# The first batch of a fused sketch attention and squared-ReLU FFN, prepared in another order

## The chip, the cores and the metric

The kernel runs on one core of one Trainium2 chip. The metric is the device time of one execution in microseconds. Three executions of the kernel before gave 197.81, 198.57 and 199.13 us; the median is 198.57.

## The reference

Attention with polynomial-sketch features, then a feed-forward layer on every token. B = 4 batches, 4 heads, 1088 tokens, head size 32, sketch size r = 8 (so 64 features), d_ff = 2048; all inputs are float32.

```python
def phi(x):
    a = np.einsum('rd,bhsd->bhsr', S1, x)
    b = np.einsum('rd,bhsd->bhsr', S2, x)
    return np.einsum('bhsi,bhsj->bhsij', a, b).reshape(*x.shape[:-1], r * r)
q_p, k_p = (phi(q), phi(k))
kv = np.einsum('bhsf,bhsd->bhfd', k_p, v)
z = np.sum(k_p, axis=2)
num = np.einsum('bhsf,bhfd->bhsd', q_p, kv)
den = np.einsum('bhsf,bhf->bhs', q_p, z)[..., None] + 1e-06
x = (num / den).transpose(0, 2, 1, 3).reshape(B * S, H * D)
h = np.maximum(x @ w_in, 0.0)
out = h * h @ w_out
```

## The kernel before

A batch of 1088 tokens is 34 tokens on each of 32 partition rows of a head; all four heads lie side by side on 128 partitions. Tokens are worked on in two groups of 512 (g = 0, 1) and a rest of 64. A group has four tiles t of 128 tokens.

**Attention of a group.** DVE turns k or q in 32x32 blocks (`turned`, L251; here with a strided output, so that a row of the result tile is token 4 s' + j). TensorE projects the turned tile with the sketches of all heads (`proj`, L265 into `ab_ps`): sixteen instructions for a group, since each float32 product is two passes and each tile two halves of 64 columns. ACT copies the factors to SBUF (`ab`, L275). `outer` (L347) multiplies the two factors into 64 features a head, on DVE or POOL (`ph_k`, `ph_q`). For k, features and v give the sums kv and z. For q, the features are turned on TensorE (`t_ps`, L1042) and evicted (`phTh`), and `numerators` (L265 into `nd`) multiplies them with the block-diagonal sums `kvbd`; its last column of each head is the denominator. `normalize` divides, scales each token by its largest value and gives x as float16 (`xs`); TensorE turns it (`x_ps`, L617) and ACT or DVE evicts it to `xT`.

**Sums.** There are two ways in the kernel. `Kv` (L389, first batch only) has the features stationary, 64 columns, and streams v with a column of ones beside it: kv and z come out in the place that `kvbd` needs, two ACT copies finish it. `KvRows` (L428, batches 1 to 3) has v stationary, 32 columns, and streams the features. Here z comes from 18 small products of the factors themselves (L447); kv and z then need further products (with the identity L478, with `pick` L485), ACT copies into `kvbd` (L492), and three DVE steps (`own_z` L497, L504).

**FFN.** The tokens of a group (a chunk) pass through 16 column blocks of w_in: `pg` (L906, float16, one pass), relu and square on DVE, ACT or POOL, then `po` (L994, float32, two passes) adds up over the 16 blocks. A finished `po` is turned back, scaled and stored (`store_gen`, L862; the store L886 is one SP transfer of 256 KB).

**Order.** The program of each engine is written out by hand. The first batch's first group is prepared line by line (L1003 to L1100); from there on `block` emits one `pg` and one `po` at a time, and `pump` lets the generators of the later work (`x_gen`, `batch_gen`, `second_gen`, `store_gen`) put their pieces between the blocks by estimated due times (`now` counts blocks). Each engine runs its own program in order. All loads and stores are on the SP queue, in order; for batches 1 to 3 q's factors pass through DRAM on it as well (`q_one`, `q_two`, `f`; L305 to L322), and POOL multiplies them to features (L332).

**PSUM.** Four tags of two banks each: `pg`, `po` and `ms` are two buffers, `nd` is one of double size. A tile of a tag waits until the readers of the tile that had the buffer are done.

**Zero products.** `idle_products(n)` (L237) issues n float16 products of zeros of 128x512 that nothing reads. In the preparation there are 17: six at the start, one behind the turn of the sketches (`s_ps`, L1005, from which DVE makes the projection weights `w_bd`, L1008), two ahead of the first group's sums, one between these and q's turn, two and five around the turn of the second group's q.

The preparation in its order on TensorE: zero products, `s_ps`, projections of k (two groups and the rest) and of q (group 0), sums of k group 0, turn of half of q's features, sums of group 1 and rest, turn of the other half, projection of q's group 1, numerators of group 0, turn of half of group 1's features, turns of `xs`, turn of the other half, first two `pg` (`first_two`, L931), numerators of group 1, two more `pg`, and the first `po`.

Of the kernel before, what the change touches and what calls it, by code (L numbers as in the profile page):

```python
# [21 lines left out]
def kernel(  # L22
# [32 lines left out]
    Identity = mybir.ActivationFunctionType.Identity  # L55
# [65 lines left out]
    def load_v(b, h, eng):  # L121
        eng.dma_start(
            v_sb[b][:, 256 * h : 256 * h + 256],
            bass.AP(
                v.tensor,
                v.offset + (b * H + h) * S * D,
                [[NM * D, 32], [8 * D, 4], [1, 256]],
            ),
        )

    def load_v_rest(b, i, eng):
        eng.dma_start(
            _v(v_rm[b // 2], 0, [[D, H], [1, D]], 64 * (b % 2) + 32 * i, 32),
            bass.AP(
                v.tensor,
                v.offset + (b * H * S + 32 + i) * D,
                [[NM * D, 32], [S * D, H], [1, D]],
            ),
        )
# [29 lines left out]
    for i in range(4):  # L169
        load_v(0, i, sp)  # L170
    load_q(0, 1)
    for i in range(2):
        load_v_rest(0, i, sp)
# [5 lines left out]
    for i in range(4):  # L179
        load_v(1, i, sp)  # L180
    for i in range(2):
        load_v_rest(1, i, sp)
# [9 lines left out]
    eps = cpool.tile([128, 1], F32)  # L192
    dve.memset(eps[:], 1e-6)
# [26 lines left out]
    def sum_constants():  # L220
        yield 1, 0
        dve.tensor_reduce(
            out=pick_s[:, :], in_=_v(iden, 0, [[1, 32], [32, 4]]), axis=AX, op=add
        )
        yield 1, 0
        pool.tensor_copy(
            out=_v(pick, 0, [[8, 32], [1, 8]]), in_=_v(pick_s, 0, [[1, 32], [0, 8]])
        )
        dve.tensor_reduce(
            out=_v(own_j, 0, [[8, 2], [1, 8]]),  # L230
            in_=_v(iden, 0, [[64, 2], [1, 8], [8, 8]]),
            axis=AX,
            op=add,
        )

# [10 lines left out]
    def turned(x, g, of_q=False):  # L246

        if g < 2:
# [3 lines left out]
                _v(xt, 0, [[128, 4], [1, 4], [4, 32]]), _v(x, c0, [[32, 4], [w, 4], [1, 32]])  # L252
# [16 lines left out]
    def proj(xt, ps_tag="ms"):  # L269
# [5 lines left out]
        act.copy(ab[:, :], ab_ps[:, :])  # L275
# [64 lines left out]
    def outer(ph, ab, t0, m, eng, a=None, g=None):  # L340


        if g is None:
            a, b, n, c0, c1 = ab if a is None else a, ab, 16, 64 * t0, 64 * t0 + 8
        else:
            a, b, n, c0, c1 = ab, ab, 8, 128 * g + 32 * t0, 256 + 128 * g + 32 * t0
        eng.tensor_tensor(  # L347
            out=_v(ph, 256 * t0, [[64, 4 * m], [8, 8], [1, 8]]),
            in0=_v(a, c0, [[n, 4 * m], [1, 8], [0, 8]]),
            in1=_v(b, c1, [[n, 4 * m], [0, 8], [1, 8]]),  # L350
            op=mult,
        )
# [11 lines left out]
    def proj_rests(xk, b, xqs, qf=None, ps_tag="ms"):  # L364
# [11 lines left out]
        for g, _ in xqs:  # L376
            act.copy(qf[64 * g : 64 * g + 64, 512:576], ab_ps[64 * g : 64 * g + 64, 64:128])

    def outer_rest(b, eng):
# [4 lines left out]
            in0=_v(ab, 0, [[8, 4], [1, 8], [0, 8]], p0, 64),  # L384
# [4 lines left out]
    class Kv:  # L389

        def __init__(self, b):
            self.b, self.n = b, 0
            self.ps = pspool.tile([128, 512], F32, name="kv_ps", tag="nd", bufs=1)

        def products(self, ph, c0, vt, v0, v1, one, p0=0, n=128):
            z = 64
            for h in range(H):
                off = v0 + v1 * h
                for f in range(0, 64, z):
                    x = 64 * (h % 2) + f  # L400
                    nc.tensor.matmul(  # L401
                        self.ps[x : x + z, 64 * (h // 2) : 64 * (h // 2) + 64],
                        ph[p0 : p0 + n, c0 + 64 * h + f : c0 + 64 * h + f + z],
                        _v(vt, off, [[one - off, 2], [1, D]], p0, n),
                        start=self.n == 0 and h < 2,
                        stop=False,
                        skip_group_check=True,
                    )
            self.n += 1

        def tiles(self, ph, g, ts):
            for t in ts:
                self.products(ph, 256 * t, v_sb[self.b], D * (4 * g + t), 256, VONE)

        def rest(self):
            r, p0 = self.b // 2, 64 * (self.b % 2)
            self.products(rest_ab[r][1], 0, v_rm[r], 0, D, H * D, p0, 64)

        def finish(self, engs):
            u = self.b  # L420
            for x in range(2):
                evict(
                    engs[x],
                    _v(kvbd[u], VW * x, [[2 * VW, 2], [1, VW]], 64 * x, 64),
                    _v(self.ps, 0, [[64, 2], [1, VW]], 64 * x, 64),
                )

    class KvRows:  # L428
# [3 lines left out]
        def __init__(self, b, abs_):  # L432
# [13 lines left out]
        def factors(self, ab, c0, c1, w, p0, n, first, last):  # L446
            nc.tensor.matmul(  # L447
                self.ps[32 * w : 32 * w + 32, 512:544],
                ab[p0 : p0 + n, c0 : c0 + 32],
                ab[p0 : p0 + n, c0 + c1 : c0 + c1 + 32],  # L450
                start=first,
                stop=last,
            )

        def products(self, phs):
            r, p0 = self.b // 2, 64 * (self.b % 2)
            for g in range(2):
                for t in range(4):
                    self.values(
                        phs[g], 256 * t, v_sb[self.b], D * (4 * g + t), 256,  # L460
                        0, 128, g + t == 0, False,
                    )
                for t in range(4):
                    self.factors(
                        self.abs, 128 * g + 32 * t, 256, t, 0, 128, g == 0, g == 1 and t > 0
                    )
            self.values(rest_ab[r][1], 0, v_rm[r], 0, D, p0, 64, False, True)
            self.factors(rest_ab[r][0], 0, 32, 0, p0, 64, False, True)
            rows = apool.tile([128, 64], F32, name="kvr", tag="kvr")
            sums = apool.tile([128, 32], F32, name="kvz", tag="kvz")  # L470
            act.copy(rows[:, :], self.ps[:, 0:64])
            act.copy(sums[:, :], self.ps[:, 512:544])
            self.rows, self.sums = rows, sums

        def spread(self):
            t_ps = pspool.tile([128, 512], F32, name="kvt_ps", tag="ms", bufs=2)
# [6 lines left out]
            for pr in range(2):  # L483
                for x in range(2):
                    nc.tensor.matmul(  # L485
                        t_ps[64 * x : 64 * x + 64, 64 + 16 * pr : 80 + 16 * pr],
                        pick[:, 128 * pr + 64 * x : 128 * pr + 64 * x + 64],
                        self.sums[:, 16 * pr : 16 * pr + 16],
                    )
            u = self.b  # L490
            for x in range(2):
                act.copy(  # L492
                    _v(kvbd[u], VW * x, [[2 * VW, 2], [1, D]], 64 * x, 64),
                    _v(t_ps, 0, [[D, 2], [1, D]], 64 * x, 64),
                )
            own_z = apool.tile([128, 32], F32, name="own_z", tag="own_z")
            dve.tensor_tensor(  # L497
                out=_v(own_z, 0, [[16, 2], [1, 16]]),
                in0=_v(t_ps, 64, [[16, 2], [1, 16]]),
                in1=_v(own_j, 0, [[0, 2], [1, 16]]),  # L500
                op=mult,
            )
            for x in range(2):
                dve.tensor_reduce(  # L504
                    out=_v(kvbd[u], VW * x + D, [[2 * VW, 2]], 64 * x, 64),
                    in_=_v(own_z, 0, [[16, 2], [1, 16]], 64 * x, 64),
                    axis=AX,
                    op=add,
                )

    def feature_t(ph, T, pr, eng):

        feat_until[0] = now[0] + 2
        t_ps = pspool.tile([128, 512], F32, name="t_ps", tag="ms", bufs=2)
        for t in range(T):
            nc.tensor.transpose(
                t_ps[:, 128 * t : 128 * t + 128],
                ph[:, 256 * t + 128 * pr : 256 * t + 128 * pr + 128],
                iden[:, :],
            )  # L520
        sb = apool.tile([128, 512], F32, name="phT", tag=f"phT{pr}", bufs=2)
        if eng is None:
            return sb, t_ps
        evict(eng, sb[:, 0 : 128 * T], t_ps[:, 0 : 128 * T])
        return sb

    def numerators(b, phT, by_pair=False):


        def cols(pr, t):  # L530
            if isinstance(phT[pr], tuple):
                return phT[pr][t // 2], 128 * (t % 2)
            return phT[pr], 128 * t

        nd = pspool.tile([128, 1024], F32, name="nd", tag="nd", bufs=1)
        steps = [(t, pr) for t in range(4) for pr in range(2)]
# [546 lines left out]
    for _ in range(2):  # L1083
        next(norm)
# [69 lines left out]
```

## Time and profile before

| | us |
|---|---|
| median of three executions | 198.57 |
| the profiled execution | 199.0 |
| its span | 197.2 |
| around the span | 1.8 |

| engine | busy us | share of the span | instructions |
|---|---|---|---|
| TensorE products (PE) | 191.5 | 97% | 1402 |
| TensorE weight loads (PEld, beside the products) | 102.7 | 52% | 1402 |
| DVE | 120.5 | 61% | 264 |
| ACT | 112.5 | 57% | 221 |
| POOL | 64.0 | 32% | 84 |

Busy time of PE is from the start of a product to its modelled end, and products overlap, so it says that the array is never long without work, not how fast it works. The speed is read from the distance of equal products. The costliest groups are the FFN's: 256 `po` instructions and 142 `pg`. In the chain that ended last, `po` has 56% of the span, `pg` 16%, `nd` 5%, `ab_ps` 3%. A timeline row is: start, duration, engine, line, operation, output and inputs, shapes, count; several instructions of a kind are one row. In brackets is the idle time of the engine ahead of it and what ended that.

### The profile page before, as it was taken

To read this page: it belongs to the slowest core of one execution; us is meant where nothing else is said; L and a number is where in the kernel's file an instruction comes from. 1 tells how busy PE (TensorE), PEld (TensorE's weight loads), DVE (VectorE), ACT (ScalarE), POOL (GpSimd) and SP (SyncE) were. 2 spreads that over 40 slices of the span, in tenths; PEclk is the share of its full clock that TensorE was granted. 3 is DMA by queue.
4 is the path that set the end of the run, shared out by engine and by line. 5 is a ranking of instruction groups with operands and counts; after the bars stand their busy time and mean duration, and the time that the engine had idled before them with its cause. 6 is when DMAs were issued, how large, how long until landed. Compare 5 with 4: busy or idle time off the path is not lost.

```text
span 197.2 us, 3669 instructions
## 1 busy us (share of the span) xinstructions
PE 191.5 (97%) x1402; PEld 102.7 (52%) x1402; DVE 120.5 (61%) x264; ACT 112.5 (57%) x221; POOL 64.0 (32%) x84
## 2 busy tenths in 40 slices
PE   7999999999999999999999999999999999999992
PEld 2784544555545454555554645455545444544791
DVE  4837897565587738547977264556387545545671
ACT  3235767663666666464757474557466656565570
POOL 3604224635245018241632271516313222222000
PEclk9999999999999999999999999999999999999999
DMA  5799840395990105982000159721000100100011
GB/s 159 217 341 326 279 128 2 83 269 165 267 327 34 56 3 130 294 240 99 2 5 0 55 118 303 193 98 53 2 0 3 53 0 0 53 0 2 0 57 27
DMA packets 13634, 21.91 MB, mean 111 GB/s; under 512 B 2672, under 2 KB 8048, under 8 KB 13616
## 3 DMA queue, kind: packets, MB, share of 16 engines
q1 hardware_dynamic: 13376, 21.60, 36.6%
q8 instruction: 11, 0.18, 0.4%
q10 hardware_dynamic: 240, 0.07, 0.2%
q14 instruction: 7, 0.06, 0.1%
HBM read 15.61 MB, written 6.06 MB: 110 GB/s over the span
## 4 chain that ended last, share of the span: by engine, by line
PE 94%; DMA 2%; DVE 1%; issue 1%; ACT 0%
PE po L994 56%; PE pg L906 16%; PE nd L265 5%; PE ab_ps L265 3%; PE kvr_ps L438 2%; PE po L953 2%; PE o_ps L871 2%; PE po_r L953 2%; DMA k_sb<-in_k_dram 2%; PE kv_ps L401 1%; PE x_ps L617 1%; PE ab_ps L282 1%; PE t_ps L1042 1%; PE idle_ps L240 1%; PE abr_ps L265 0%
## 5 line engine op out<-in xcount | busy, mean ns | idle before, releaser
L994 PE MATMUL po<-g,w_o 128*128 128x512 f32 x256 | 130.6, 592 | 0.0
L923 DVE TENSOR_SCALAR gt<-pg 128x512 f32<-128x512 f32 (+1 forms) x107 | 69.2, 651 | 52.5 <-PE pg L906 38.1
L926 ACT ACTIVATE g<-gt 128x512 f32<-128x512 f32 (+1 forms) x107 | 63.8, 598 | 58.8 <-DVE gt L923 56.4
L994 PEld LDWEIGHTS po<-g,w_o 128*128 128x128 f32 x256 | 48.5, 191 | 35.7 <-issue 19.2
L914 POOL TENSOR_TENSOR g<-gt 128x512 f32<-128x512 f32 x23 | 23.9, 1040 | 79.3 <-ACT gt L913 79.3
L906 PE MATMUL pg<-xT,w_in 128*128 128x512 f16 x126 | 47.8, 380 | 0.0
L906 PEld LDWEIGHTS <-w_in 128*128 128x128 f16 x142 | 13.8, 98 | 25.0 <-issue 24.1
L332 POOL TENSOR_TENSOR phF<-f,f 128x576 f32<-128x576 f32 (+1 forms) x12 | 16.1, 1364 | 12.8 <-DMA f<-q_two 12.8
L347 POOL TENSOR_TENSOR ph_k<-ab 128x512 f32<-128x512 f32 x14 | 14.5, 1070 | 10.1 <-ACT ab L288 8.8
L913 ACT ACTIVATE gt<-pg 128x512 f32<-128x512 f32 x23 | 13.4, 581 | 0.0
L879 DVE TENSOR_TENSOR o_sb<-o_ps,beta 128x512 f32<-128x512 f32 x8 | 5.5, 692 | 6.9 <-PE o_ps L871 6.9
L251 DVE STREAM_TRANSPOSE xt<-k_sb 128x512 f32<-128x512 f32 x8 | 8.6, 1117 | 1.7 <-DMA k_sb<-in_k_dram 1.7
L265 PEld LDWEIGHTS nd<-kvbd,phF 128*64 128x64 f32 x208 | 6.9, 137 | 4.5 <-issue 4.5
L251 DVE STREAM_TRANSPOSE xt<-q_sb 128x512 f32<-128x512 f32 x8 | 8.6, 1121 | 0.0
L265 PEld LDWEIGHTS ab_ps<-w_bd,xt 128*64 128x64 f32 x160 | 7.1, 163 | 2.5 <-issue 1.2
L265 PE MATMUL ab_ps<-w_bd,xt 128*64 128x64 f32 x160 | 7.5, 252 | 0.4 <-DVE w_bd L1008 0.4
L920 ACT ACTIVATE g<-gt 128x512 f32<-128x512 f32 x12 | 7.6, 630 | 0.4
L240 PE MATMUL idle_ps<-zero 128*128 128x512 f16 x17 | 6.6, 511 | 1.2 <-DVE own L198 1.2
L265 PE MATMUL nd<-kvbd,phF 128*64 128x66 f32 x208 | 7.7, 224 | 0.0
L919 ACT ACTIVATE gt<-pg 128x512 f32<-128x512 f32 x12 | 7.0, 587 | 0.0
L953 PE MATMUL po<-w_o,g 128*128 128x128 f32 x32 | 6.2, 278 | 0.0
L953 PE MATMUL po_r<-w_o,g 128*128 128x128 f32 x32 | 6.0, 275 | 0.0
(114 smaller groups left out, 143.4 us busy)
## 6 DMA issues: line engine op xcount, KB each, us to landing
q_two<-qf SPq DMA_DIRECT2D x8, 288.0 KB, 4.1
f<-q_one SPq DMA_DIRECT2D x4, 576.0 KB, 6.1
f<-q_two SPq DMA_DIRECT2D x4, 576.0 KB, 4.7
v_sb<-in_v_dram SPq DMA_DIRECT2D x16, 128.0 KB, 4.0
out_dram<-o_sb SPq DMA_DIRECT2D x8, 256.0 KB, 2.4
k_sb<-in_k_dram SPq DMA_DIRECT2D x3, 544.0 KB, 6.1
q_sb<-in_q_dram SPq DMA_DIRECT2D x3, 544.0 KB, 4.4
w_in<-in_moe_w_in_dram SPq DMA_DIRECT2D x2, 512.0 KB, 6.2
```

Source lines behind the costliest of these rows:

```text
L240: nc.tensor.matmul(idle_ps[:, :], zero[:, 0:128], zero[:, :])
L251: dve.transpose(_v(xt, 0, [[128, 4], [1, 4], [4, 32]]), _v(x, c0, [[32, 4], [w, 4], [1, 32]]))
L265: nc.tensor.matmul(out_ps[p0 + c : p0 + c + z, c0 : c0 + w], lhsT[:, l0 + c : l0 + c + z], rhs)
L332: pool.tensor_tensor(out=ph[:, c], in0=fs[g][0][:, c], in1=fs[g][1][:, c], op=mult)
L347: eng.tensor_tensor(out=_v(ph, 256 * t0, [[64, 4 * m], [8, 8], [1, 8]]), in0=_v(a, c0, [[n, 4 * m], [1, 8], [0, 8]]), in1=_v(b, c1, [[n, 4 ...
L906: nc.tensor.matmul(pg[:, 0:nt], w_in[:, 128 * c : 128 * c + 128], xT[:, 0:nt])
L913: act.activation(gt[:, 0:nt], pg[:, 0:nt], Relu)
L914: pool.tensor_tensor(out=g2[:, 0:nt], in0=gt[:, 0:nt], in1=gt[:, 0:nt], op=mult)
L923: dve.tensor_scalar(out=gt[:, 0:nt], in0=pg[:, 0:nt], scalar1=0.0, scalar2=None, op0=amax)
L926: act.activation(g2[:, 0:nt], gt[:, 0:nt], Square)
L953: nc.tensor.matmul(po[r][:, 0:128], g2[:, 128 * r : 128 * r + 128], w_o[:, 128 * c : 128 * c + 128], start=c == 0, stop=c == NC - 1,)
L994: nc.tensor.matmul(po[0][:, 0:nt], w_o[:, 128 * c : 128 * c + 128], g2[:, 0:nt], start=(c == 0), stop=(c == NC - 1),)
```

## The change

It rewrites the preparation of the first batch and, with it, the order of tokens inside a tile.

- Zero products: seven and two (for six and one) up to the first projection; the two and the one ahead of and between the sums are gone; four and two (for two and five) stand around the turn of the second group's first half.
- The first batch's sums are made by `KvRows`: z from the factors, picked out early (`pick_sums` into a tile of the tag `po`, `own_sums` on DVE), kv from 72 products with v stationary, then `turn` and `place`. The constants for it (`pick`, `own_j`) are made in the setup and no longer in a lane of the later work.
- ACT's copy of the factors puts the two factors apart (`ab`), as for the later batches. `outer` and `outer_rest` on DVE take one factor from PSUM.
- q is turned without stride: a row of the tile is token s' of 32, in four runs. So the store of a chunk becomes four transfers of 64 KB.
- The numerators of group 0 are two tiles, `nd` and `nd_b` (tag `pg`), and `normalize_first` works on both; the denominator's small sum is on DVE, where it was on ACT.
- Of group 1, only the first half of the features is turned ahead of the first FFN products; the second half is turned behind the first four, and its numerators are put into the stream of blocks by a lane that starts at block 2.
- Two of the four casts of w_in (for three) come ahead of the first FFN products.

```diff
@@ turned, proj
             dve.transpose(
-                _v(xt, 0, [[128, 4], [1, 4], [4, 32]]), _v(x, c0, [[32, 4], [w, 4], [1, 32]])
+                xt[:, :] if of_q else _v(xt, 0, [[128, 4], [1, 4], [4, 32]]),
+                _v(x, c0, [[32, 4], [w, 4], [1, 32]]),
             )
...
-        act.copy(ab[:, :], ab_ps[:, :])
+        act.copy(
+            _v(ab, 0, [[128, 2], [8, 16], [1, 8]]), _v(ab_ps, 0, [[8, 2], [16, 16], [1, 8]])
+        )
@@ sums
+    def factor_sums(ps, c0, ab, a0, a1, w, p0, n, first, last):
+        nc.tensor.matmul(
+            ps[32 * w : 32 * w + 32, c0 : c0 + 32],
+            ab[p0 : p0 + n, a0 : a0 + 32],
+            ab[p0 : p0 + n, a0 + a1 : a0 + a1 + 32],
+            start=first,
+            stop=last,
+        )
+    def pick_sums(t_ps, c0, sums):
+        for pr in range(2):
             for x in range(2):
+                nc.tensor.matmul(
+                    t_ps[64 * x : 64 * x + 64, c0 + 16 * pr : c0 + 16 + 16 * pr],
+                    pick[:, 128 * pr + 64 * x : 128 * pr + 64 * x + 64],
+                    sums[:, 16 * pr : 16 * pr + 16],
                 )
...
@@ normalize_first
+        for i, nd in enumerate(nds):
+            dve.tensor_reduce(
+                out=_v(top, 8 * i, [[4, 2], [1, 4]]),
+                in_=_v(nd, 0, [[256, 2], [VW, 4], [1, 32]]),
+                axis=AX, op=amax, apply_absolute_value=True,
+            )
+            dve.tensor_scalar(
+                out=den[:, 8 * i : 8 * i + 8], in0=_v(nd, D, [[256, 2], [VW, 4]]),
+                scalar1=1e-6, scalar2=None, op0=add,
+            )
+        dve.reciprocal(rden[:, :], den[:, :])
...
+        for i, nd in enumerate(nds):
             dve.tensor_tensor(
+                out=_v(xs, 256 * i, [[128, 2], [32, 4], [1, 32]]),
...
@@ store_gen
-        sp.dma_start(dst, o_sb[:, :])
+        for dst, p0, n, c0, w in dsts:
+            sp.dma_start(dst, _v(o_sb, c0, [[1, w]], p0, n))
@@ the preparation
-    idle_products(6)
+    idle_products(7)
     s_ps = pspool.tile([128, 16], F32, name="s_ps", tag="nd", bufs=1)
     nc.tensor.transpose(s_ps[:, :], s_nat[:, :], iden[0:16, 0:16])
-    idle_products(1)
+    idle_products(2)
...
-    xk.append(turned(k_sb[0], 2))
-    xq = turned(q_sb[0], 0, True)
     pk = [proj(xk[0], "pg"), proj(xk[1], "pg")]
-    proj_rests(xk[2], 0, [])
-    pq = proj(xq)
...
+    xkr = turned(k_sb[0], 2)
+    xq = turned(q_sb[0], 0, True)
     for g in range(2):
         outer(phk[g], pk[g][1], 0, 2, dve, pk[g][0])
         outer(phk[g], pk[g][1], 2, 2, pool)
-    idle_products(2)
-    kv0 = Kv(0)
-    kv0.tiles(phk[0], 0, range(4))
+    pq = proj(xq)
+    pkr = proj_rests(xkr, 0, [])
+    kv0 = KvRows(0)
+    for g in range(2):
+        for t in range(4):
+            factor_sums(kv0.ps, 512, pk[g][1], 32 * t, 128, t, 0, 128, g == 0, g == 1 and t > 0)
+    kv0.rest_sums()
+    kv0.keep_sums()
     outer(phq, pq[1], 0, 2, dve, pq[0])
+    outer_rest(0, dve, pkr)
     outer(phq, pq[1], 2, 1, dve, pq[0])
     outer(phq, pq[1], 3, 1, pool)
-    outer_rest(0, dve)
-    idle_products(1)
+    zt_ps = pspool.tile([128, 32], F32, name="zt_ps", tag="po", bufs=2)
+    pick_sums(zt_ps, 0, kv0.sums)
+    for g in range(2):
+        for t in range(4):
+            kv0.tile(phk[g], g, t)
+    own_sums(0, zt_ps, 0)
+    xq1 = turned(q_sb[0], 1, True)
...
-    turned_half(0, (act, act))
-    xq1 = turned(q_sb[0], 1, True)
-    kv0.tiles(phk[1], 1, range(4))
-    kv0.rest()
-    kv0.finish((act, act))
-    turned_half(2, (act, dve))
+    pqT = [turned_half(phq, 0, (act, act))]
+    kv0.rest(True)
+    kv0.keep_rows()
+    pqT.append(turned_half(phq, 2, (act, dve)))
+    kvt_ps = pspool.tile([128, 64], F32, name="kvt_ps", tag="pg", bufs=2)
+    kv0.turn(kvt_ps)
+    kv0.place(kvt_ps)
+    nd_b = pspool.tile([128, 512], F32, name="nd_b", tag="pg", bufs=2)
+    nd0 = [
+        numerators(0, pqT[0], None, range(2)),
+        numerators(0, pqT[1], nd_b, range(2, 4)),
+    ]
     pq1 = proj(xq1, "pg")
     phq1 = ph_tile("ph_q", 2)
-    outer(phq1, pq1[1], 0, 2, pool)
-    nd0 = numerators(0, pqT)
-    idle_products(2)
...
+    for t0 in (0, 2):
+        outer(phq1, pq1[1], t0, 2, pool)
...
+    idle_products(4)
+    pqT = [turned_half(phq1, 0, (act, act))]
+    idle_products(2)
+    chunk_of(0, 0, xT0, next(norm))
     first_two()
-    nd1 = numerators(0, pqT1, True)
+    nd1 = numerators(0, pqT[0], None, range(2))
     nd_taken[0] = True
     for _ in range(2):
         first_product()
-    act.copy(w_in[:, 1536:2048], w_in32[:, 1536:2048])
+    pqT.append(turned_half(phq1, 2, (act, dve)))
+    for c in range(2, 4):
...
+    def second_half():
+        numerators(0, pqT[1], nd1[:, 512:1024], range(2, 4))
+        yield 1, 0
+        yield from x_gen(0, 1, None, (), nd1)
+
+    lanes.append([second_half(), 2, 1])
...
-    lanes.append([x_gen(0, 1, None, (), nd1), 3, 1])
-    lanes.append([sum_constants(), 8, 0])
```

In `KvRows`, `tile` and `rest` are the 64 and 8 instructions of the 72, `rest_sums` the last factor sums, `keep_rows` and `keep_sums` ACT's copies of kv and z out of PSUM, `turn` the products with the identity and `place` ACT's two copies into `kvbd`.

## The prediction

> **What bounds it now.** I read the windows by stage first, then the chain of waits of the first 23 us, then the timeline of the same stretch by engine. The windows (stretch, its length, busy time and instructions of PE, PEld and so on) split the run in two:
>
> ```profile
> 0.00:19.00 19.00, 17.05 (x208) 10.85 (x208) 11.30 (x34) 6.88 (x18) 6.87 (x23) 1.00 0.83 257
> 21.10:60.00 38.90, 38.90 (x280) 19.55 (x280) 27.30 (x56) 24.40 (x48) 15.77 (x18) 1.00 0.63 186
> 130.00:170.00 40.00, 40.00 (x161) 19.43 (x160) 23.39 (x53) 24.24 (x43) 11.48 (x13) 1.00 0.04 14
> ```
>
> From the first `po` product (21.09) on TensorE has no hole; every other engine rests 30% of it or more. So that part is as long as its TensorE work, and the change can gain only where the first batch is prepared. The chain (start, us, what) shows that preparation:
>
> ```profile
> 5.09 2.10 PE ab_ps L265 x32
> 7.40 1.00 PE ab_ps L265 x16
> 8.40 0.97 PE idle_ps L240 x2
> 9.36 1.29 PE kv_ps L401 x32
> 10.65 0.32 PE idle_ps L240
> 11.41 1.46 PE kv_ps L401 x40
> 14.07 0.96 PE nd L265 x32
> 15.06 0.28 ACT small L560
> 19.04 0.59 PE pg L936 x2
> 19.63 1.08 PE nd L265 x32
> 21.25 0.92 PE po L994 x2
> ```
>
> Up to 15 us it runs through TensorE, zero products (`idle_ps`) included; then through DVE's normalization to the first FFN product at 19.04. TensorE's own timeline (start, us, engine, line) says at what speed:
>
> ```profile
> 1.19 2.74 PE L240 MATMUL idle_ps<-zero 128*128 128x512 f16 x6 [1.19 <-DVE own L198]
> ...
> 7.27 1.12 PE L265 MATMUL ab_ps<-w_bd,xt 128*64 128x64 f32 x16
> ...
> 13.39 0.69 PE L265 MATMUL ab_ps<-w_bd,xt 128*64 128x64 f32 x16
> ...
> 16.18 1.24 PE L240 MATMUL idle_ps<-zero 128*128 128x512 f16 x5
> ...
> 43.30 0.65 PE L438 MATMUL kvr_ps<-ph_k,v_sb 128*32 128x64 f32 x32
> ```
>
> Six zero products take 2.74 us at the start, five take 1.24 later; sixteen projection products take 1.12, later 0.69. The page's clock row shows full speed throughout, but the spacing says half speed at first. The products of `kv_ps` in windows of 0.2 us place the change at about 9.8:
>
> ```profile
> 9.48:9.68 0.20, 0.20 (x8) 1.00 0.82 164
> 9.68:9.88 0.20, 0.20 (x10) 1.00 0.91 225
> 9.88:10.08 0.20, 0.20 (x14) 1.00 0.64 205
> ```
>
> **The change, part by part.** *Zero products at the start.* Seven instead of six end at 1.19 + 7 x 0.43 = 4.2. The S transpose moves from 3.86 to 4.3 and is hidden: `w_bd` waits anyway for DVE's first transpose (4.84). Two zero products behind it end at 5.35, so the first projection starts at about 5.5 instead of 5.09: +0.4. What it may buy is the clock. Now TensorE pauses for about 1 us in all between 3.7 and 6.1; with the change for about 0.5. I take full speed at 6.4 (bounds: 5, and 9.8 as now).
>
> *To the features.* First projection 5.5 to 6.35 at half speed, plus 0.3 until its last result: ACT's copy 6.66 to 7.03 (now 6.26 to 6.63). POOL, which follows at once,
>
> ```profile
> 6.72 2.09 POOL L347 TENSOR_TENSOR ph_k<-ab 128x512 f32<-128x512 f32 x2 [1.25 <-ACT ab L275]
> 8.89 0.62 POOL L347 TENSOR_TENSOR ph_q<-ab 128x256 f32<-128x256 f32 x1
> ```
>
> then ends its two `ph_k` halves at 9.2 and its `ph_q` quarter at 9.9; 0.4 later than now. DVE is not later: it turns k and q until 7.07 now, and begins its first `ph_k` half there. The q turn without stride: the contiguous 128x64 k rest takes 232 ns, the strided q rest 232, the strided 128x512 turn 1121; nearest contiguous row of 512 columns is `gt`, 691. So 0.69 to 1.12; I take 0.7 as that row has the shape. Neither end enters the sum, because the first `ph_k` half waits for the copy at 7.03 in both, and the seven other q turns lie on an engine with a third of its time free. [...]
>
> Second projection at full speed 6.4 to 7.05, third 6.95 to 7.55 (0.69 each, row 13.39), copy at 7.95. DVE: `ph_k` 7.07 to 8.33 (1.26 as now), `ph_q` (0.63, then 0.37) and the rest (0.37) to 9.75, where now they end at 10.2. With the clock late: 10.3.
>
> *Sums.* Removed: 72 `kv_ps` products, 1.29 + 1.46 = 2.75 us, and three zero products (8.40 and 10.65, 1.29 us) in front of them. Added: 72 products with v stationary (two times 0.65, which overlap their neighbours: the whole group in batch 1 runs from 43.30 to 44.74, its 18 factor sums included: 1.44), 8 picking and 4 turning products (0.36 and 0.34 by batch 3's rows, tails included). The factor sums wait for ACT's copies (8.2), the picking for `keep_sums` (8.7); the 64 big ones run 9.0 to 9.9, behind the last `ph_k` half at 9.2. Then `ph_q`'s turn: its PSUM buffer is now the one of the q projection, so all of the DVE products at 9.75 must be over; start 10.1. From there 4 turns (0.44), 8 rest products, ACT's two evictions and `keep_rows` (0.65 + 0.21) to 11.4, `kv0.turn` to 11.85, two `place` copies (0.42) to 12.3. This last piece is new (before: two copies out of `kv_ps`). `own_sums` (0.19 + 2 x 0.18) and xq1's turn lie on DVE between 9.75 and 11.4, under ACT's chain; without that cover they cost up to 1.3. So the numerators start at 12.35 instead of 13.90; late clock 12.6.
>
> *Normalization.* `nd` in two tiles: the second half ends at 13.5 (half of 0.96 each); DVE starts its first reduction at 13.05. Left behind the last product: 0.42 reduction, 0.2, reciprocal and five small steps at 0.2 to 0.28 (now 16.04 to 17.15 for five of them), two `xs` halves at 0.4: 2.8, where now 15.03 to 18.28 = 3.25. `xs` is complete at 16.35. On TensorE xq1's projection now follows the numerators: copied at 14.4, so POOL's two products (1.06 and 1.07) are at 15.5 and 16.6. The turn of the first half and two zero products stand before the `xs` turns, so these start at 16.55, 0.2 behind `xs`. Evictions as now (0.37, 0.29), first FFN product at 17.35: -1.7.
>
> *Behind it.* Now 2.05 us pass from there to the first `po`, filled by 32 numerators; then 16 numerators, two products that wait for their buffers (relu at 1.3 us behind the first product) and the second half's turns (0.44), 2.3 us: first `po` at 19.65, -1.45. The 16 numerators left are moved into block 2, where TensorE is the bound: half of 1.08, plus about 0.1 (a group of 32 adds 1.19 between blocks at 50.85 to 52.26): +0.65. Sum: -1.45 + 0.65 = **-0.8**; late clock -0.55.
>
> *Stores, loads and constants.* Eight stores of 0.59 us issue time become 32; a piece costs 0.35 to 0.59 (shortest and ordinary SP rows), so a store takes 0.8 to 1.8 us longer on SP. Behind the one at 44.12 stand the second group's factor transfers: `f` lands at 51.3 + 4.7 = 56.0 and POOL uses it at 57.92; 1.9 us of cover, then 1.2 more until the numerators at 61.96. Costed at nothing; with the cover gone up to 1. The last store is `o_row`, unchanged. Picking constants lie in DVE's wait for k (1.71 us before 3.90, they take 0.74).
>
> **Rivals** (times from the profiled 199.0). *The clock falls back* (slower). Between 7.5 and 12.3 TensorE would have about 2.3 us of work, 48%, and no zero products; the emptiest stretch at full speed now, 15 to 19, has some 55%, five zero products among it. For it: lower than anything the trace shows held. Against: no pause is longer than about 1 us. It decides if the array is slow again at the numerators: these and turns +1.2, then blocks of 1.07 at double length. The start needed 8.6 us of mixed work to reach full speed; 2 to 4.3 us of loss: +2.4 to +4.7 net, 201.4 to 203.7. [...]
>
> *A wait at block 2.* The moved numerators need ACT's eviction of the second half, queued behind two squares: ready at about 21.5, TensorE there at 21.6. Half to one us late, with all later `po` queued behind: -0.3 to +0.2, 198.7 to 199.2.
>
> *Clock at 5:* the first projection too is full speed, POOL 0.35 earlier: -1.1 to -1.3, 197.7 to 197.9.
>
> **Numbers.** The profiled execution took 199.0 (span 197.2, 1.8 around it); the median shown is 198.57, so against the median every result lies 0.43 lower. Forecast 0.52: 198.57 - 0.7 (between -0.55 and -0.8) = 197.9, own range 197.4 to 198.4. Wait at block 2: 0.2. Early clock: 0.15. Clock falling back: 0.13 by the trace (almost all that is over 1% slower). Range 196.9 to 199.8: the early clock with the early end of its terms, and the wait with a store's lost cover. About 1% (2 us) is what can be told from no change. Faster by more needs nearly three times my sum: 0.08; slower 0.12.
>
> **What would show it.** Right: first projection near 5.5 with sixteen products in 0.7 us by the second; numerators near 12.4, first FFN product near 17.4, first `po` near 19.7, no holes after. Wrong: `po` pitch over 1.07 near 20 (clock), idle TensorE before the numerators in block 2, DVE still busy with `own_sums` or xq1 at 12.3, or POOL waiting for `f` near 58.

## The result and the profile after

The changed kernel takes 199.31 us (median of 20 executions, 199.01 to 199.71); the kernel before, measured beside it, 197.81 (20 executions, 197.52 to 199.28). The ratio is 1.0062, with a 95% interval of 1.0047 to 1.0077: 0.6% slower, where 0.35% faster was forecast. (It is the ratio of the means, 199.31 and 198.08. The medians lie further apart, because the kernel before has a group of six executions above 198.3 and fourteen at 197.98 or below.) The profiled execution of the changed kernel took 199.55, its span is 197.8. (Executions more than 1.5% above the fastest of their kernel are left out of all ratios here, but not out of medians.)

TensorE's timeline after (start, duration, engine, line, operation, output and inputs, shapes, count, and in brackets the idle time ahead with what ended it) has these rows for the steps that the prediction names:

```profile
5.47 2.26 PE L257 MATMUL ab_ps<-w_bd,xt 128*64 128x64 f32 x48
...
12.66 0.69 PE L257 MATMUL nd<-kvbd,phTh 128*64 128x66 f32 x16 [0.53 <-ACT kvbd L487]
...
15.52 0.39 PE L231 MATMUL idle_ps<-zero 128*128 128x512 f16 x1 [0.48 <-issue]
...
17.42 0.61 PE L575 MATMUL x_ps<-iden,xs 128*128 128x128 f16 x4 [0.43 <-DVE xs L564]
18.51 0.59 PE L942 MATMUL pg<-xT,w_in 128*128 128x512 f16 x2 [0.47 <-DVE xT L76]
...
20.53 1.02 PE L1000 MATMUL po<-g,w_o 128*128 128x512 f32 x2
...
22.56 1.02 PE L257 MATMUL nd<-kvbd,phTh 128*64 128x66 f32 x16
```

The preparation did become shorter than in the first profile: the first `po` starts at 20.53, where it was 21.09. But more than half of the 1.24 gained up to the numerators (12.66, before 13.90) is lost again between them and the first FFN product (18.51, before 19.04: 0.53 left), and the rest at the 16 numerators in block 2 (blocks are counted from 0, so this is the third). There are 128 blocks of the kind `po`, of two instructions each. Setting the first instruction of each against that of the same block in the first profile gives -0.55 for the first block, -0.62 for the second, +0.44 for the third and +0.48 for the last. So the 125 blocks behind the third, with all the stores in four pieces, lost 0.04 together.

The normalization is seen in DVE's timeline after:

```profile
14.89 0.17 DVE L549 TENSOR_REDUCE mm<-small 128x4 f32<-128x16 f32 x1
15.10 0.77 DVE L553 TENSOR_SCALAR mp<-mm 128x4 f32<-128x4 f32 x1
15.91 0.18 DVE L556 RECIPROCAL rm<-mp 128x4 f32<-128x4 f32 x1
16.12 0.79 DVE L557 TENSOR_TENSOR small<-small,rm 128x16 f32<-128x16 f32 x1
```

and POOL's timeline over the same stretch has this row for its two products:

```profile
14.78 2.09 POOL L344 TENSOR_TENSOR ph_q<-ab 128x512 f32<-128x512 f32 x2 [5.01 <-ACT ab L267]
```

Two steps of 128x4 and 128x16 elements take 0.77 and 0.79 us, while steps of the same size next to them take 0.17 or 0.18. The first ends (15.87) where POOL's first product ends (15.85), the second (16.91) where POOL's second does (16.87). The bracket of neither row names a wait: it lies inside the duration. In the profile before, the first of these steps (`mp`) lay between POOL's two products and took 0.17:

```profile
16.73 0.17 DVE L578 TENSOR_SCALAR mp<-mm 128x4 f32<-128x4 f32 x1
```

```profile
14.57 1.06 POOL L347 TENSOR_TENSOR ph_q<-ab 128x512 f32<-128x512 f32 x1 [5.05 <-ACT ab L275]
...
17.13 1.07 POOL L347 TENSOR_TENSOR ph_q<-ab 128x512 f32<-128x512 f32 x1
```

### The profile page after: what moved, and what is told of

The parts are those of the page before. It is cut to its first block, busy times and chain, and to the rows that moved or that the text cites. A ratio compares the mean times of both kernels' runs of the same rounds, so it can differ in the third digit from the quotient of the medians.

```text
span 197.8 us, 3764 instructions
## 1 busy us (share of the span) xinstructions
PE 190.1 (96%) x1430; PEld 101.3 (51%) x1430; DVE 119.7 (61%) x267; ACT 113.0 (57%) x224; POOL 63.9 (32%) x84
## 4 chain that ended last, share of the span: by engine, by line
PE 92%; DVE 3%; ACT 1%; issue 1%; POOL 1%
PE po L1000 55%; PE pg L912 15%; PE nd L257 4%; PE ab_ps L257 3%; PE kvr_ps L433 3%; PE idle_ps L231 2%; PE po L959 2%; PE o_ps L876 2%; PE po_r L959 2%; PE ab_ps L276 1%; PE x_ps L620 1%; PE t_ps L1058 1%; PE kvt_ps L479 1%; POOL g L950 1%; DVE small L538 0%
## 5 line engine op out<-in xcount | busy, mean ns | idle before, releaser
L231 PE MATMUL idle_ps<-zero 128*128 128x512 f16 x15 | 6.0, 530 | 1.7 <-DVE own L195 1.2
L257 PEld LDWEIGHTS ab_ps<-w_bd,xt 128*64 128x64 f32 x160 | 6.5, 152 | 2.0 <-issue 0.9
L257 PE MATMUL ab_ps<-w_bd,xt 128*64 128x64 f32 x160 | 6.5, 237 | 0.0
L876 PEld LDWEIGHTS o_ps<-iden,oT 128*128 128x128 f32 x32 | 3.9, 141 | 3.9 <-issue 2.9
```

Source lines behind the costliest of these rows:

```text
L231: nc.tensor.matmul(idle_ps[:, :], zero[:, 0:128], zero[:, :])
L257: nc.tensor.matmul(out_ps[p0 + c : p0 + c + z, c0 : c0 + w], lhsT[:, l0 + c : l0 + c + z], rhs)
```

## The experiments

In each profile the trace records from when on TensorE's clock is granted in full; "onset" is that time. With it go the starts of the first numerators, of the first FFN product and of the first `po`.

| kernel | onset | numerators | `xs` complete | first FFN product | first `po` | span |
|---|---|---|---|---|---|---|
| before, first profile | 9.78 | 13.90 | 18.28 | 19.04 | 21.09 | 197.2 |
| before, again | 4.96 | 13.11 | 17.48 | 18.24 | 20.29 | 196.4 |
| before, zero products 7 and 2 | 6.42 | 12.54 | 16.91 | 17.67 | 19.72 | 195.9 |
| after | 6.91 | 12.66 | 17.69 | 18.51 | 20.53 | 197.8 |
| after, again | 6.12 | 13.11 | 18.14 | 18.96 | 20.98 | 198.2 |
| after, second product on DVE | 6.00 | 12.56 | 16.98 | 17.80 | 19.94 | 197.0 |
| after, xq1 early | 6.76 | 12.60 | 16.78 | 18.22 | 20.24 | 197.5 |
| after, both | 4.30 | 12.37 | 16.18 | 17.14 | 19.28 | 196.4 |
| after, operands in PSUM | 6.85 | 12.63 | 16.45 | 17.76 | 19.78 | 197.0 |
| after, evictions exchanged | 6.02 | 12.86 | 17.89 | 18.71 | 20.73 | 197.6 |
| after, zero products 6 and 1 | 5.26 | 12.61 | 17.64 | 18.46 | 20.49 | 197.7 |
| all cures | 6.96 | 12.81 | 16.65 | 21.30 | 23.36 | 199.7 |
| all cures, loads later | 5.14 | 13.04 | 16.88 | 17.86 | 19.91 | 196.1 |
| the same, v rest first | 4.78 | 12.31 | 16.15 | 17.43 | 19.48 | 195.6 |

**The kernel before once more** (no edit).

> The kernel before, unchanged, for a second profile of it. Theory A (the profile that the prediction was made from shows a late run): in about two of three executions TensorE reaches full speed well ahead of 9.8 us, the numerators start near 12.9 and the span is near 196.0. Rival B: the executions differ elsewhere (transfers, end), and the start looks as in the first profile (full speed near 9.8, numerators 13.9) whatever the span.

It took 198.21. TensorE's timeline:

```profile
13.11 1.11 PE L265 MATMUL nd<-kvbd,phTh 128*64 128x66 f32 x32
...
20.29 1.08 PE L994 MATMUL po<-g,w_o 128*128 128x512 f32 x2
```

The same program is 0.8 us earlier from the numerators to its end. So the profile that the prediction was made from was an execution with a late onset, and of the 1.24 us between numerators at 13.90 and at 12.66 a large part (0.8 here) is not the change's work. Loads differ from execution to execution too: here DVE's second turn of k began at 5.17, behind a wait of 0.20 for its load, where with seven and two zero products (below) it began at 4.75 without one. An onset alone therefore does not give the time of an execution.

**The changed kernel again** (no edit).

> The changed kernel, unchanged, for its time beside the experiments and a second profile. From the first `po` on it should stand as in the first profile: 1.0 to 1.1 us lost at the third `po` block against the kernel before, nothing later. Where TensorE reaches full speed between 4.3 and 8 us, the span is 197.2 to 197.8 and the time 199.0 to 199.6.

199.64, ratio 1.0072 (1.0041 to 1.0104); the slowdown repeats on another chip, and both long DVE steps with it (0.78 and 0.79).

**xq1's second product on DVE, behind the first group's normalization.** With that POOL has only one product under way while DVE takes its small steps.

```diff
-    for t0 in (0, 2):
-        outer(phq1, pq1[1], t0, 2, pool)
+    outer(phq1, pq1[1], 0, 2, pool)
...
     chunk_of(0, 0, xT0, next(norm))
+    outer(phq1, pq1[1], 2, 2, dve)
```

> The changed kernel, with POOL's second feature product of q's group 1 given to DVE, behind the eviction of x. Theory A (small DVE steps whose operands all lie in SBUF wait for a POOL product under way): the step that took 0.79 us (scale of each token) takes 0.17 again, the step at 0.77 (mp) stays long as the first product is still there; first FFN product 0.5 to 0.7 earlier, time 0.4 to 0.6 below the changed kernel's (198.8). Rival B (the turns and evictions ahead of x bind): no change, 199.3.

198.85, ratio 1.0021 (0.9997 to 1.0044). The second long step is at 0.17 again, the first stays at 0.77: one step for each POOL product. `xs` is complete 0.7 earlier than after, at numerators 0.1 earlier.

**xq1's projection ahead of the numerators**, so that POOL begins earlier.

```diff
     kv0.place(kvt_ps)
+    pq1 = proj(xq1, "pg")
...
-    pq1 = proj(xq1, "pg")
```

> The changed kernel, with the projection of q's group 1 ahead of the numerators, in TensorE's hole before them. Both POOL products then run from 13.1 to 15.2. Theory A: mp and the scale step are short (0.17 each), and the first step with two SBUF operands (rtop) waits until 15.2 instead, 0.5 us; time 0.6 to 0.8 lower, 198.6. Rival B (turns and evictions bind): the turn of the first half and its evictions come 1.2 us earlier and the gain comes although the DVE steps stay long. Rival C: neither binds, 199.3.

199.11, ratio 1.0030 (1.0001 to 1.0058). Now another DVE step meets POOL, the product of the largest values with the reciprocal (0.54 for 0.17, to 15.16), and the two long ones are short. `xs` is complete at 16.78; but the first FFN product is only at 18.22, for a reason that was not expected. TensorE stands still between its zero products:

```profile
13.69 0.82 PE L231 MATMUL idle_ps<-zero 128*128 128x512 f16 x3
16.16 0.39 PE L231 MATMUL idle_ps<-zero 128*128 128x512 f16 x1 [1.65 <-issue]
```

A zero product waits for nothing that the program names. The profile after has the same hole (0.48, at 15.52), where it was hidden: the turn behind it had to wait for POOL's first product (15.85) in any case.

**Both edits together.**

> Both of the last two edits. Theory A: no DVE step of the normalization is above 0.3 us except those on 128x256, x complete near 16.5 instead of 17.7; first FFN product 1.1 to 1.2 earlier, time near 198.2. If the waits are not POOL's doing, no more than the larger of the two single gains.

199.10, ratio 1.0013 (0.9992 to 1.0034). No DVE step is long, `xs` is complete 3.81 behind the numerators' start (after: 5.03), the hole before the fourth zero product is 0.80. The median is 0.9 above the expected 198.2. The profiled execution (198.19) is the fastest of the twelve, so what the others lose is not seen.

**Two small operands in PSUM.** The reciprocal `rden` and the largest value `mm` lie in a free corner of `nd`, so that no small DVE step has all its operands in SBUF. POOL's work is not touched.

```diff
-        dve.reciprocal(rden[:, :], den[:, :])
+        rden, mm = nds[0][:, 512:528], nds[0][:, 544:548]
+        dve.reciprocal(rden, den[:, :])
```

> The changed kernel, with two small tiles of the first normalization (the reciprocal of the denominators and the largest value) in a free corner of the PSUM tile `nd` and not in SBUF. POOL's two products stay where they are. [...]

199.22, ratio 1.0041 (1.0014 to 1.0068). DVE's timeline, and under it POOL's:

```profile
15.08 0.16 DVE L554 TENSOR_SCALAR mp<-nd 128x4 f32<-128x4 f32 x1
15.28 0.18 DVE L557 RECIPROCAL rm<-mp 128x4 f32<-128x4 f32 x1
15.49 0.17 DVE L558 TENSOR_TENSOR small<-nd,rm 128x16 f32<-128x16 f32 x1
```

```profile
14.74 2.09 POOL L344 TENSOR_TENSOR ph_q<-ab 128x512 f32<-128x512 f32 x2 [4.97 <-ACT ab L267]
```

POOL is as busy as before and the steps are short: 0.16 and 0.17. So DVE had waited for POOL (0.77 and 0.79 in the profile after), and what decided whether these two steps waited was where their operands lie. The reduction and the reciprocal in between, each from SBUF to SBUF, did not wait beside POOL's products even in the profile after (0.17 and 0.18). Why the place of the operands matters, the traces do not show. The gain did not all arrive: `xs` was 1.24 earlier, the first FFN product 0.75. TensorE's own order now ends last: the turn of `ph_q` waits for POOL's first product until 15.87, two zero products stand behind it, and the turns of `xs` start at 16.79, 0.34 after `xs` is complete.

**DVE evicts the first part of the second half, ACT the other.**

```diff
-    pqT.append(turned_half(phq1, 2, (act, dve)))
+    pqT.append(turned_half(phq1, 2, (dve, act)))
```

> The changed kernel, with DVE evicting the first and ACT the second part of the second half's turned features. Theory A (the moved numerators wait in block 2 for two evictions, one behind the other): DVE starts near 21.6 and ACT near 22.2, numerators without a hole; the loss at the third `po` block falls from 1.06 to 0.7 to 0.8, time 0.25 to 0.35 lower. Rival B: ACT's part comes last anyway, behind its squares, and nothing changes (within 0.1).

199.18, ratio 1.0043 (1.0023 to 1.0062). In TensorE's timeline the numerators in block 2 are

```profile
22.76 0.69 PE L257 MATMUL nd<-kvbd,phTh 128*64 128x66 f32 x16
```

instead of 1.02 with a hole of 0.28 in it, and against the first profile the `po` behind them lose 0.72, not 1.06. So 0.34 of block 2's price was the wait for the evictions, and 0.72 the products themselves.

**All cures at once**: operands in PSUM, xq1's projection early, the rest sums and the turn of kv early, DVE evicting first in the second half of group 0, and all 32 numerators of group 1 behind the first FFN products as in the kernel before (its second half is turned ahead of them and evicted by ACT, so block 2 has none). Only the edit for the numerators is shown.

```diff
-    pqT = [turned_half(phq1, 0, (act, act))]
+    pqT = [turned_half(phq1, t0, (act, act)) for t0 in (0, 2)]
...
     nd1 = numerators(0, pqT[0], None, range(2))
+    numerators(0, pqT[1], nd1[:, 512:1024], range(2, 4))
```

> The changed kernel with what the theories ask for: the two tiles in PSUM, xq1's projection in the hole ahead of the numerators, the rest's sums and `keep_rows` ahead of q's turn, DVE first in the second eviction, and both halves of group 1's features turned ahead of the first FFN product, all 32 numerators behind it as in the kernel before. Sum of the theories against the changed kernel: normalization -1.2, block 2 -1.06, kv path -0.3: 196.9 to 197.3 where that one has 199.3; below the kernel before by 0.5 or more at a like start. If the DVE steps or the turns bind elsewhere, at least the block-2 part, -1.0, remains.

198.50 (197.74 to 202.17), ratio 1.0001 (0.9972 to 1.0030): the loss is gone in most executions, but three of twelve are above 200. The profiled one is among them. Its windows (stretch, length, busy time and instructions of PE, granted clock, DMA share, GB/s) and TensorE's timeline show why:

```profile
10.40:14.60 4.20, 3.99 (x71) 1.00 1.00 344
14.60:17.20 2.60, 0.07 (x1) 1.00 0.99 327
17.20:20.60 3.40, 3.30 (x15) 0.50 0.80 223
```

```profile
17.30 0.61 PE L231 MATMUL idle_ps<-zero 128*128 128x512 f16 x1 [2.63 <-issue]
17.70 1.91 PE L1061 MATMUL t_ps<-iden,ph_q 128*128 128x128 f32 x8
```

The hole has grown to 2.63 us, and behind it the clock is at half for 3.4 us: eight turns take 1.91, where they take 1.04 in the last kernel below. This is what the rival "the clock falls back" had forecast, but behind a pause that the prediction did not have. One profile shows it.

What goes with the hole can be read from the trace's records of single packets. All of TensorE's recorded instructions are counted here, 2886 in the changed kernel: products, weight loads, and 26 semaphore and drain instructions. The packet is the first of 16 KB on the instruction queue q8 within the run.

| kernel | 193rd instruction | packet | 449th instruction | the next one |
|---|---|---|---|---|
| before | 10.81 | 13.81 to 14.85 | 19.85 | at once |
| after | 9.35 | 12.98 to 14.02 | 14.66 | 15.52 |
| after again | 9.11 | 13.23 to 14.27 | 15.11 | 15.68 |
| second on DVE | 9.20 | 13.23 to 14.18 | 14.55 | 15.48 |
| xq1 early | 9.28 | 13.53 to 14.95 | 14.13 | 16.15 |
| both | 9.05 | 12.64 to 13.61 | 13.90 | 15.07 |
| operands in PSUM | 9.32 | 12.89 to 13.87 | 14.62 | 15.10 |
| evictions exchanged | 9.02 | 13.09 to 14.65 | 14.85 | 15.95 |
| zero products 6 and 1 | 9.31 | 13.65 to 14.62 | 15.85 | 16.11 |
| all cures | 9.37 | 14.91 to 15.86 | 14.29 | 17.30 |

The pause of the changed kernels in this table is always behind the 449th instruction and ends 1.2 to 1.5 us after the packet has landed. What stands there made no difference: with two zero products fewer (last experiment below) the 450th instruction belongs to a turn of `ph_q`, and the four zero products run without a hole. Eleven such packets come within the run, 262 recorded instructions to a packet. In the profile after, nine of the ten later ones start within 22 instructions of the 193rd plus a multiple of 256 (at the 471st, 710th, 949th, 1209th and so on), the first one only behind the 369th. All this fits one account, which is the author's estimate from these times: TensorE had run out of program. Its next piece was asked for at about the 193rd instruction, 256 ahead, and came 3.6 to 5.5 us later. In the kernel before, 9 us lie between the 193rd and the 449th instruction; in the changed one 4.8 to 6.5. So in the kernel before the packet had landed (14.85) 5.0 us ahead of the 449th instruction (19.85), and there is no pause. That q8 serves TensorE, and what a packet holds, the trace does not say.

**The same with the loads later.** The loads that are not needed at once (w_out, batch 1, q's rest) are put behind a small DVE write at 9.3 us, to take them out of the way of that packet.

```diff
-    load_w_o(0)
...
-    load_rest(q_sb[0], q, 0)
...
     outer(phq, pq[1], 3, 1, pool)
+    dve.tensor_copy(w_o[:, 0:1], pq[1][:, 0:1])
+    load_w_o(0)
...
+    load_rest(q_sb[0], q, 0)
```

> The version before this one (all cures at once), with one more edit: the loads that batch 0's first group does not need before its first po product (both halves of w_out, all of batch 1, the rests) are issued behind DVE's product of ph_q (about 9.7 us) instead of at 8.0 to 17. Theory A (instruction supply): in every kernel with the change, TensorE stands still between the third and the fourth of four zero products, always at its 449th or 450th recorded instruction, and goes on 2.3 to 2.9 us after the start of a 16 KB packet of the instruction queue; that packet comes 3.2 to 5.5 us after TensorE's 193rd instruction (256 earlier), because the loads stand ahead of it. With the loads later, the packet starts at 12 or before, the pause is under 0.3 (was 2.63 in the profile before this one, 0.8 in the kernel with both edits), the first FFN product is at 16.3 to 16.8, the first po at 18.5 to 19.0, and no slow stretch follows; the median is 197.2 to 198.0, 0.6 to 1.2 below the kernel before on the same chip, and no execution above 200. Theory B (the pause has nothing to do with the loads): the pause stays at 0.8 or more, the median is within 0.3 of the kernel before, and some executions stay above 200.

197.55 (197.11 to 198.46), kernel before on the same chip 198.59, ratio 0.9957 (0.9937 to 0.9976). The packet came at 12.09 to 13.26 and the zero products have no hole:

```profile
10.84 0.32 PE L423 MATMUL kvr_ps<-phr_k,v_rm 64*32 64x64 f32 x8 [0.69 <-DMA v_rm<-in_v_dram]
...
14.08 1.04 PE L221 MATMUL idle_ps<-zero 128*128 128x512 f16 x4
```

The median is as theory A had it; that the later loads brought the packet forward is not shown by it (see the next run). The first FFN product is not (17.86, not 16.3 to 16.8): v's rest, on the same queue, landed late and cost 0.69 ahead of the numerators.

**v's rest ahead of q's second group** in that version.

```diff
+    for i in range(2):
+        load_v_rest(0, i)
     load_q(0, 1)
-    for i in range(2):
-        load_v_rest(0, i)
```

> The version with the later loads, with batch 0's v rest issued ahead of q's second group instead of behind it. In that version's profile TensorE waited 0.69 for this load ahead of the eight rest products, and the numerators began at 13.04. Theory A: the rest products follow the first 64 without a pause, the numerators begin at 12.4 to 12.6 at a like onset of the clock, and the first FFN product is 0.2 to 0.5 earlier than 17.86; the median is 0.2 to 0.4 below the 197.55 of that version's chip, against the kernel before a ratio of 0.993 to 0.995. Rival: the first FFN product hangs on xq1's projection and POOL's two products, which hang on q's second group, now later: ratio within 0.001 of 0.9957, or above.

197.31 (196.99 to 198.04), kernel before on the same chip 198.45, ratio 0.9948 (0.9926 to 0.9971): by its median the fastest kernel of this study, though its interval overlaps that of the version before it. The numerators are at 12.31 without a wait, slightly better than expected. But the hole came back:

```profile
14.93 0.39 PE L221 MATMUL idle_ps<-zero 128*128 128x512 f16 x1 [0.76 <-issue]
15.16 1.04 PE L1061 MATMUL t_ps<-iden,ph_q 128*128 128x128 f32 x8
```

The packet started at 12.63, 3.47 behind the 193rd instruction; the version before this one had 2.96, all profiles of changed kernels with early loads 3.58 to 5.54. That would fit the view that loads delay the packet, but 3.47 and 3.58 are too close to settle it, and the three profiles with the old preparation, whose loads are early too, have 3.00, 3.72 and 4.09. So it stays open what delays the packet. What the profiles do show is that the hole ends 1.2 to 1.5 us behind it.

**Zero products: the kernel before with seven and two.**

```diff
-    idle_products(6)
+    idle_products(7)
...
-    idle_products(1)
+    idle_products(2)
```

> The kernel before with seven and two zero products instead of six and one, nothing else. Theory A: the two more zero products cost 0.4 us at the first projection (5.5 instead of 5.1) and buy a full clock at 7 us or earlier in every execution, where the kernel before had it at 9.8 in one profile and 5.0 in another; so the executions lie closer together: none above 198.9 apart from odd ones, the lower end 0.2 to 0.4 above that of the kernel before, median within 0.4 of it. Rival: the clock does not depend on them; the profile may show an onset later than 7.5, and the executions keep the width of those of the kernel before, all 0.4 later.

197.88 (197.68 to 198.15, twelve executions), kernel before on the same chip 198.59, ratio 0.9972 (0.9956 to 0.9989). Beside it eleven of 23 executions of the kernel before lie at 197.80 to 198.20 and twelve at 198.59 to 199.16: the upper group is gone, the lower one not worse. TensorE's timeline:

```profile
5.47 1.57 PE L265 MATMUL ab_ps<-w_bd,xt 128*64 128x64 f32 x32
...
12.54 1.11 PE L265 MATMUL nd<-kvbd,phTh 128*64 128x66 f32 x32
...
19.72 1.08 PE L994 MATMUL po<-g,w_o 128*128 128x512 f32 x2
```

With this one item of the change, the old preparation has its numerators at 12.54, where the new one has them at 12.66 and, in its second profile, at 13.11. All its `po` are 1.37 earlier than in the first profile. Not all of that need be the clock: k's first load also came earlier in this execution (DVE's first turn at 3.65, not 3.90). On this chip the version with the later loads has 197.55, so all the rest of the work, cures included, is worth 0.3 us beside these two zero products.

**Zero products: the changed kernel with six and one** (the reverse edit).

> The changed kernel with six and one zero products up to the first projection, as the kernel before has them, instead of seven and two. [...]

200.62 from only six executions, in two groups: 199.53 to 199.66 and 201.58 to 202.99; ratio 1.0110 (1.0058 to 1.0163). Two groups, as in the 23 executions of the kernel before beside the last run, but 1.9 us lie between them, where 0.4 lie between those. The profile is of the lower one (onset 5.26); what the upper ones lost was not seen.

## Why the prediction was wrong

| step | predicted | measured |
|---|---|---|
| first projection | 5.5 | 5.47 |
| full clock | 6.4 (5 to 9.8) | 6.91; 4.30 to 6.96 in the others with 7 and 2 |
| ACT's first copy | 6.66 | 6.64 |
| POOL's `ph_k` done | 9.2 | 9.19 |
| q's turn without stride | 0.7 | 0.71 |
| `ph_q` turned from | 10.1 | 10.29 |
| numerators from | 12.35 | 12.66 |
| `xs` complete | 16.35 | 17.69 |
| first FFN product | 17.35 | 18.51 |
| first `po` | 19.65 | 20.53 |
| 16 numerators in block 2 | +0.65 | +1.06 |
| stores | 0 | 0.04 with all else behind block 2 |

*First failed step: what the clock was worth.* "With the clock late" moved the sum only from -0.8 to -0.55, so the clock had a price of 0.25, and the kernel before was taken to have it late always ("9.8 as now"). The experiment with seven and two in the kernel before gave 1.37 against the same profile. Up to 0.25 of this may be k's load, and the second profile of the kernel before, with its onset at 4.96, gained 0.80; its two groups of executions lie 0.9 apart. By each of these the price, in the kernel before, is at least three times what was assumed. (In the changed kernel itself it was not measured: no profile of it has a late onset.) So the gain of 1.55 that the sum had at the numerators was not the work of the new sums: without the 2.75 us of `kv_ps` products the numerators are at 12.66, with them, and with the zero products alone, at 12.54. And since half or more of the executions of the kernel before are of the lower group (14 of 20 in the first comparison, 11 of 23 beside the zero products), a gain counted from one late execution could not be taken over to the median by subtracting 0.43. That the lower group is the one with the early onset is seen in two profiles only.

*Second: the normalization.* "Five small steps at 0.2 to 0.28" were counted; two of them took 0.77 and 0.79, 1.22 more together, because POOL's two products were moved to lie beside them. From the numerators to `xs` the sum had 4.0 us, and 5.03 were measured. The prediction placed POOL's products nearly rightly (ends at 15.5 and 16.6; measured 15.85 and 16.87), but used them only as a condition for TensorE's turns. In the kernel before, POOL's second product came behind `beta`, and DVE's `xs` steps beside it (L600) read PSUM. It is the largest single miss in the sum: with the operands in PSUM the first `po` is 0.75 earlier at a like onset. Alone it does not decide the sign, since that version is still above the kernel before (1.0041).

*Third: block 2.* The moved products cost 0.72, near the 0.65 of the sum; the rival "a wait at block 2" came true in part, at 0.34, by the queue on ACT that it named. The rival "the clock falls back" did not come true in the changed kernel itself (20 executions within 0.7 us); it was seen in the version with all cures, after a pause of 2.63 us for which the prediction had no cause, as it knew only waits for data.

In the prediction's own sum, the first `po` gained 0.55 and not 1.45: the numerators were 0.31 late and the normalization 1.03 too long, while the two stretches behind it were 0.18 and 0.28 shorter than assumed, which hid part of the miss. Block 2 cost 1.06 and not 0.65, the rest 0.04. So -0.8 became +0.5 against the first profile. The median of the kernel before, 197.81 where 198.57 had been shown, did the rest.

Against the kernel before with a like onset (6.42, 6.91), the whole of the change but the zero products cost 1.85: 0.12 up to the numerators, 0.66 in the normalization (the 1.22 of waits, less 0.56 that its two parts did save), about 0.04 to the first `po`, 1.03 behind it. (The 0.12 is less than the 0.45 by which the two profiles of the changed kernel differ at that point.) Costed rightly were the start, POOL's chain, the turn of q, the chain to kvbd within 0.3, and the stores.

## What to carry to other kernels

Take more than one profile of a kernel whose preparation runs while TensorE's clock is still rising: here the same program differed by 0.8 us (onset 9.78 and 4.96), more than the effect that was forecast, and two dummy products, alone, came within 0.3 us of the version of the rewrite that was measured beside them. When work is moved to POOL or in time, list the DVE steps beside it that read only SBUF; here two tiny ones lasted until POOL's instruction ended (0.77 and 0.79 us), and an operand in PSUM freed them (0.16 and 0.17). Look for "issue" idle time at a fixed instruction number: here it took 0.2 to 2.6 us behind the 449th in the faster preparation, and the author's estimate is that TensorE outran the supply of its own program.

## What the runs showed of the hardware

- The full clock came at 4.3 to 9.8 us in the fourteen profiles, and its recorded stretches are multiples of 3.41 us (187.73, 55 of them, or 191.15, 56 of them, in thirteen profiles; 10.24, then 3.41 at half, then 177.49 in the other, the one with all cures).
- A DVE TENSOR_SCALAR of 128x4 from SBUF to SBUF and a TENSOR_TENSOR of 128x16 with two operands in SBUF lasted until the POOL product beside them ended (0.77 and 0.79 for 0.17); with an operand in PSUM they did not (0.16 and 0.17). A reduction to 128x4 and a reciprocal of 128x4 from SBUF to SBUF did not either (0.17 and 0.18).
- In every profile of a changed kernel but that of all cures with loads later, TensorE stood still behind its 449th recorded instruction, for 0.2 to 2.6 us, until 1.2 to 1.5 us after a 16 KB packet of the instruction queue had landed; the longest pause was followed by 3.41 us at half speed.
- DVE's turn of 128x512 float32 took 0.67 to 0.73 with a contiguous output (profile after) and 1.06 to 1.18 with a strided one (profiles before and after).
